# The split words of w_val and w_out come back on SyncE's queue, under a newly searched order table

## The chip, the cores and the metric

The kernel runs on one core of a Trainium2 chip. The metric is the device time of one execution in microseconds, as the median of the runs shown; a profiled execution is a run of its own. Engines are named as in the profile: PE (matmul), PEld (its weight load), DVE (VectorE), ACT (ScalarE), POOL (GpSimd) and SP (SyncE, which here only issues transfers).

## What is computed

Windowed attention feeds a channel mix with squared ReLU and a sigmoid gate, and that feeds a gated projection whose gate is a causal convolution of five taps. All is float32 outside; the weights come in as float64.

```python
# q, k, v: (4, 8, 576, 64)
scores = q @ k^T / sqrt(64), kept where 0 <= row - col < 64
x = softmax(scores) @ v                         # to (4, 576, 512)
xk = mu_k * x + (1 - mu_k) * x_prev;  xr = mu_r * x + (1 - mu_r) * x_prev
v = relu(xk @ w_k) ** 2 @ w_v                   # 512 -> 1024 -> 512
x = sigmoid(xr @ w_r) * v
gate = sigmoid(sum over k of conv_w[k] * xp[:, k:k + S, :])
out = (gate * (x @ w_val)) @ w_out
```

## The kernel before

**Stages.** The 2304 tokens (4 batches of 576) are cut into block 0 of 256 and blocks 1 to 4 of 512. For each block the attention of four head pairs (units) is computed, then the mix: `r` (4 tiles of 128 columns), `h` (8 tiles) and `v` (4 tiles). Results of a block are stored to `x2d` in device memory (`st`). The last stage goes by batch: it loads x of a batch (`ldx`, tile `xb`) and the batch's gate (`ldg`, tile `gate`), multiplies by `w_val` (`val`) and by `w_out` (`out`).

**Split words.** A float32 product is made of three faster ones: both sides are split into a high word and a low word, and high x high, high x low and low x high are summed. A high word is a copy with rounding (`xhi_`, `ghi_`, on ACT or DVE), a low word the difference (`xlo_`, `glo_`, on DVE). In the last stage a product over quarters is made by seven instead of eight products (`m1` to `m7`; each is a group of 12 matmuls on PE), which needs sums of quarters of x and of the weights (`xsum`, tile `xt`). Batch 3's `out` is a plain product of 8 groups, so the stage has 28 + 21 + 8 = 57 groups.

**The weights of the last stage.** During blocks 3 and 4 the quarters of `w_val` and `w_out` are made into their split words (`w_val ld` to `w_val st`) and written to device memory. They come back when the room of the earlier weights is free: `wv2` loads the words of `w_val` into `wk` (after the last `h`), `wo2` those of `w_out` into `wr` (after the last `r`) and into `wol0` and `wol1`. These six loads are issued by POOL.

**Early gates.** For batches 0 to 2 the gate is computed ahead, six half batches in all: load x (`cld`), five taps for each of two column tiles (`ctap`, tile `early`, the first on ACT, the others on DVE), a sigmoid (`cgate`, ACT), store (`cst`, to `gd`).

**What sets the order.** `SLOT` is a table that gives each step a place in one order for all engines, and each engine runs its own steps in that order; a letter before a number says which engine takes a step that may run on either (`a` ACT, `v` DVE, `p` POOL). The order was found by a search with the step lengths that are written at the steps. SP runs its transfers in order too: one that waits holds those behind it. A transfer waits for the producers of its data and for the readers of the room that it fills. So `ldx` of batch 0 waits for POOL's memset of `xb`, and that of batch 1 for the end of `v` in block 4, since its room is that of `wv`.

Of the kernel before, what the change touches and what calls it, by code (L numbers as in the profile page):

```python
# [26 lines left out]
NF = DM // P  # L27
NFF = DFF // P
# [3 lines left out]
NB = len(BLOCKS)  # L32
# [1169 lines left out]
```

## Time and profile before

| what | value |
|---|---|
| median of 3 runs | 429.45 us (429.11 to 430.32) |
| the profiled execution | 432.7 us, span of its instructions 430.9 us |
| mean granted TensorE clock | 0.984 |
| busy, share of the span | PE 96%, DVE 82%, ACT 59%, POOL 4% |
| moved by the 16 DMA engines | 77.69 MB, 180 GB/s in the mean |

The span runs from the first to the last instruction; the time has something around it. Matmuls are pipelined and their ends are modelled, so a busy PE is not yet a PE at full pace.

### The profile page before, as it was taken

What the parts mean: (1) busy time and instruction counts of PE and PEld (TensorE: products, weight loads), DVE (VectorE), ACT (ScalarE), POOL (GpSimd) and SP (SyncE); (2) the same over time, 40 slices, a digit from 0 to 9 for tenths busy, and PEclk for the clock granted to TensorE, in tenths of its full rate; (3) what the DMA queues carried; (4) which work ended last, traced back from release to release, by engine and by line L of the source; (5) the groups of instructions that cost most, each with busy time, mean ns of one, the idle gap of its engine ahead of it and who ended that gap; (6) DMA issues with size and microseconds to landing.
All of it is one profiled execution on the core that took longest, in us unless ns stands there. A gap on an engine that the chain in (4) does not pass through costs nothing.

```text
span 430.9 us, 9154 instructions
## 1 busy us (share of the span) xinstructions
PE 415.3 (96%) x3744; PEld 356.5 (83%) x3744; DVE 355.4 (82%) x524; ACT 253.5 (59%) x579; POOL 19.2 (4%) x67
## 2 busy tenths in 40 slices
PE   7899999999999999999999999999993999999996
PEld 6588888888888888888888888888883999999996
DVE  4899999879987899598989899597239699999970
ACT  5899997888956487761128642334211458675731
POOL 2000000000000000000000000001100000001000
PEclk9799999999999999999999999999997899999999
DMA  7998931452331725401384473529994803607533
GB/s 276 368 418 316 364 109 50 124 181 66 138 104 57 251 76 175 136 20 50 123 300 142 180 257 146 208 106 386 364 351 151 331 1 111 192 2 193 110 140 137
DMA packets 24714, 77.69 MB, mean 180 GB/s; under 512 B 2528, under 2 KB 3296, under 8 KB 22624
## 3 DMA queue, kind: packets, MB, share of 16 engines
q1 hardware_dynamic: 23088, 66.88, 43.5%
q0 software_dynamic: 1440, 10.22, 7.5%
q8 instruction: 29, 0.48, 0.4%
q14 instruction: 13, 0.11, 0.1%
q10 hardware_dynamic: 144, 0.00, 0.0%
HBM read 53.90 MB, written 20.84 MB: 173 GB/s over the span
## 4 chain that ended last, share of the span: by engine, by line
PE 72%; DVE 19%; DMA 6%; issue 1%; ACT 1%; SPq 0%; ACTq 0%; POOL 0%; DVEq 0%; POOLq 0%
PE h L592 18%; PE v L592 15%; PE r L592 8%; DMA xb<-x2d 4%; PE at L501 4%; PE at L489 4%; PE scores L428 4%; DVE x L759 4%; PE v L615 3%; PE h L615 3%; PE out L967 3%; PE val0m L861 2%; PE out2m L861 2%; DVE early L792 2%; DVE gq L759 2%; DVE xt L749 2%
## 5 line engine op out<-in xcount | busy, mean ns | idle before, releaser
L592 PE MATMUL h<-x,wk 128*128 128x512 f32 x384 | 90.5, 392 | 0.0
L592 PEld LDWEIGHTS h<-x,wk 128*128 128x128 f32 x384 | 71.4, 188 | 14.7
L592 PE MATMUL v<-sh,wv 128*128 128x512 f32 x256 | 82.7, 394 | 0.0
L592 PEld LDWEIGHTS v<-sh,wv 128*128 128x128 f32 x256 | 48.1, 188 | 9.9
L592 PE MATMUL v<-sl,wv 128*128 128x512 f32 x128 | 49.8, 389 | 0.0
L792 DVE SCALAR_TENSOR_TENSOR early<-early,wc 128x576 f32<-128x576 f32 x48 | 38.6, 813 | 11.3 <-ACT early L790 11.1
L592 PE MATMUL r<-x,wr 128*128 128x512 f32 x192 | 45.4, 392 | 0.0
L592 PEld LDWEIGHTS r<-x,wr 128*128 128x128 f32 x192 | 35.7, 188 | 7.3
L471 ACT ACTIVATE s<-s,m 128x128 f32<-128x128 f32 x96 | 37.1, 389 | 7.1 <-DVE m L460 7.0
L592 PEld LDWEIGHTS v<-sl,wv 128*128 128x128 f32 x128 | 24.1, 188 | 4.7
L489 PE MATMUL at<-ident,s 128*128 128x128 f32 x144 | 23.8, 288 | 1.9 <-DVE s L481 1.0
L501 PEld LDWEIGHTS at<-pt,vt 128*64 128x64 f32 x576 | 19.2, 141 | 7.2 <-issue 3.4
L489 PEld LDWEIGHTS at<-ident,s 128*128 128x128 f32 x144 | 16.9, 143 | 7.2 <-issue 1.4
L501 PE MATMUL at<-pt,vt 128*64 128x64 f32 x576 | 22.2, 229 | 0.5 <-DVE pt L495 0.5
L481 DVE TENSOR_TENSOR s<-s,m 128x1024 f32<-128x1024 f32 (+1 forms) x20 | 22.3, 1114 | 0.2
L552 DVE SCALAR_TENSOR_TENSOR xm<-xT,omu,xm 128x512 f32<-128x512 f32 x32 | 22.3, 745 | 0.1
L672 DVE TENSOR_TENSOR sl<-rk,sh 128x1024 fp32r<-128x1024 f32 x16 | 19.4, 1220 | 3.2 <-ACT rk L670 3.1
L642 ACT ACTIVATE rk<-h 128x512 f32<-128x512 f32 (+1 forms) x25 | 12.8, 541 | 13.6 <-PE h L592 8.7
L861 PE MATMUL val0m<-x,wk 128*128 128x288 f32 x84 | 14.1, 333 | 7.0 <-DVE x L759 7.0
L756 ACT ACTIVATE x<-xt 128x576 fp32r<-128x576 f32 x15 | 10.1, 681 | 18.1 <-issue 11.5
L861 PEld LDWEIGHTS val0m<-x,wk 128*128 128x128 f32 x84 | 13.6, 224 | 7.4 <-DVE x L759 7.3
L575 DVE TENSOR_TENSOR x<-xm,x 128x1024 fp32r<-128x1024 f32 x16 | 19.3, 1219 | 0.2
(186 smaller groups left out, 844.7 us busy)
## 6 DMA issues: line engine op xcount, KB each, us to landing
qk<-qk SPq DMA_DIRECT2D x16, 544.0 KB, 5.3
vt<-vh SPq DMA_DIRECT2D x16, 512.0 KB, 4.7
xb<-x2d SPq DMA_DIRECT2D x4, 1152.0 KB, 7.4
out_t<-st SPq DMA_DIRECT2D x15, 288.0 KB, 2.5
x2d<-sgs SPq DMA_DIRECT2D x16, 256.0 KB, 3.4
w_out<-w SPq DMA_DIRECT2D x8, 512.0 KB, 2.6
w_val<-w SPq DMA_DIRECT2D x8, 448.0 KB, 2.6
wk<-w_val POOLq DMA_DIRECT2D x2, 1792.0 KB, 10.3
```

Of the source, the lines that this page charges most:

```text
L471: ACT.activation(out=s, in_=scores()[:, c // n2, c % n2, :] if by_pe else s, func=AF.Exp, scale=D ** -0.5 if by_pe else 1.0, bias=l(0)[:, ...
L481: lambda: V.tensor_tensor(out=a["s"], in0=a["s"], in1=l(1).unsqueeze(2).to_broadcast(sq), op=ALU.mult))
L489: PE.transpose(a["tp", h][:, c * P:(c + 1) * P], a["s"][:, h * n2 + c, :], ident)
L501: PE.matmul(a["o"][heads[h], c * W:(c + 1) * W], lhsT=a["v"][:, c, heads[h]], rhs=a["pt"][:, h, c * W:(c + 1) * W], start=True, stop=True)
L552: V.scalar_tensor_tensor(out=m, in0=xT[:, f, :n], scalar=omu[:, c:c + 1], in1=m, op0=ALU.mult, op1=ALU.add)
L575: lambda E: E.tensor_tensor(out=dst(1), in0=src(), in1=f32(dst(0)), op=ALU.subtract))
L592: PE.matmul(ps, lhsT=a, rhs=b[:, kt, :], start=(kt == 0 and i == 0), stop=(kt == nk - 1 and i == 2))
L615: PE.matmul(Ps[key][:, :n], lhsT=ws(kt), rhs=x()[:, kt, :], start=kt == 0, stop=kt == nk - 1)
L672: lambda E: E.tensor_tensor(out=Ss[t][1][:, f, :n], in0=rk(), in1=f32(Ss[t][0][:, f, :n]), op=ALU.subtract))
L759: lambda E: E.tensor_tensor(out=lo(), in0=src(), in1=f32(hi()), op=ALU.subtract))
L792: V.scalar_tensor_tensor(out=o, in0=x, scalar=c, in1=o, op0=ALU.mult, op1=ALU.add)
L861: PE.matmul(z[bank][:, j, :HS], lhsT=lhs, rhs=rhs, start=new and kt == 0 and e == 0, stop=kt == 1 and e == 2, skip_group_check=not new)
```

## The change

The six loads `wv2` and `wo2` are issued by SP in place of POOL, as copies of float32 into a float32 view of the tile. The length that the search took for the scores is 965 ns for blocks 1 to 4 and 411 ns for block 0, where it was 822 ns and half of that. With both the table was searched anew, and nearly all of its numbers differ; of these the diff shows the lines that the text speaks of.

```diff
-    'ldc': '161',
+    'ldc': '17',
...
-    'w_v hi': 'a371 a353 a307 a280',
+    'w_v hi': 'a320 v396 a437 a276',
...
-    'wv2': '870 872',
-    'wo2': '898 904 900 902',
-    'ldx': '893 943 958 1015',
+    'wv2': '891 901',
+    'wo2': '944 900 890 946',
+    'ldx': '886 942 960 1009',
...
-        op(("qk", u), "pe", 822 * nc_ // 8 + (208 if t == 0 else 241) * by_pe, [("ldqk", u), *(["low"] if by_pe else []), *([] if t else ["idle"])], qk,
+        op(("qk", u), "pe", (965 if t else 411) + (208 if t == 0 else 241) * by_pe, [("ldqk", u), *(["low"] if by_pe else []), *([] if t else ["idle"])], qk,
...
-        op(("wv2", c), "pool", 1000, stored("w_val", c) + [("h", NB - 1, m) for m in range(NFF)],
-           lambda c=c: G.dma_start(out=flat(wk[c])[:, :14 * 256], in_=flat4(wd["w_val", c])), moves=1.25 * 14 * 256)
+        op(("wv2", c), "dma", 420, stored("w_val", c) + [("h", NB - 1, m) for m in range(NFF)],
+           lambda c=c: DMA.dma_start(out=f32(flat(wk[c])[:, :14 * 256]), in_=flat4(wd["w_val", c])), moves=1.25 * 14 * 256)
         for j in range(2):
-            op(("wo2", c, j), "pool", 1000, stored("w_out", c) + ([("turn_w", j)] if c else [("r", NB - 1, m) for m in range(NF)]),
-               lambda c=c, j=j: G.dma_start(out=Q["wol", j] if c else flat(wr[j]),
+            op(("wo2", c, j), "dma", 420, stored("w_out", c) + ([("turn_w", j)] if c else [("r", NB - 1, m) for m in range(NF)]),
+               lambda c=c, j=j: DMA.dma_start(out=f32(Q["wol", j] if c else flat(wr[j])),
                                               in_=flat4(wd["w_out", c])[:, j * 2048:(j + 1) * 2048]), moves=1.25 * 2048)
```

The line numbers of the changed kernel are one higher than before from the scores on. In the order's rows `xb_3285` and `xb_3254` are x of batch 0, `xb_3452` and `xb_3451` that of batch 1.

**SP's queue from the last store of split words to x of batch 1.** Before:

```order
L1109 DMA w_out_106<-w_2608 128x1024
L779 DMA early<-x2d 128x2x576
L798 DMA gd<-early 128x2x576
L724 DMA xb_3285<-x2d 128x4x576
L808 DMA gate_3245<-gd 128x4x576
L798 DMA gd<-early 128x2x576
L697 DMA x2d<-sgs 128x512
L724 DMA xb_3452<-x2d 128x4x576
```

Now, from the store of the gate on:

```order
L799 DMA gd<-early 128x2x576
L725 DMA xb_3254<-x2d 128x4x576
L809 DMA gate_3237<-gd 128x4x576
L1121 DMA wol_3058<-w_out_106 128x2048
L1118 DMA wk_63<-w_val_103 128x3584
L1121 DMA wr_66<-w_out_105 128x2048
L1118 DMA wk_64<-w_val_104 128x3584
L698 DMA x2d<-sgs 128x512
L799 DMA gd<-early 128x2x576
L725 DMA xb_3451<-x2d 128x4x576
L1121 DMA wr_65<-w_out_105 128x2048
L1121 DMA wol_3277<-w_out_106 128x2048
```

Four of the loads stand between the gate of batch 0 and the sixth gate's store, two behind x of batch 1.

**The end of the fifth early gate, on DVE** (`early<-early,wc` is a tap, `rk<-h` a rectify, `rk<-rk` the square's product, `sl` its low word, `w<-s` the words of w_out). Before, its eight taps and what lies between:

```order
L792 SCALAR_TENSOR_TENSOR early<-early,wc 128x576 x2
L1106 TENSOR_TENSOR w_2608<-s_3046,w_2570 128x1024
L792 SCALAR_TENSOR_TENSOR early<-early,wc 128x576
L672 TENSOR_TENSOR sl<-rk,sh 128x1024
L644 TENSOR_SCALAR rk<-h_5_3147 128x512
L792 SCALAR_TENSOR_TENSOR early<-early,wc 128x576 x2
L644 TENSOR_SCALAR rk<-h_6_3184 128x512
L792 SCALAR_TENSOR_TENSOR early<-early,wc 128x576
L669 TENSOR_TENSOR rk<-rk 128x1024
```

Now, from the product of the block's first square on:

```order
L670 TENSOR_TENSOR rk<-rk 128x1024
L673 TENSOR_TENSOR sl<-rk,sh 128x1024
L793 SCALAR_TENSOR_TENSOR early<-early,wc 128x576
L1095 TENSOR_TENSOR s_3019<-s_3019 128x128
L1107 TENSOR_TENSOR w_2627<-s_2980,w_2588 128x1024
L793 SCALAR_TENSOR_TENSOR early<-early,wc 128x576
L645 TENSOR_SCALAR rk<-h_4_3112 128x512
L793 SCALAR_TENSOR_TENSOR early<-early,wc 128x576 x4
L1107 TENSOR_TENSOR w_2627<-s_3019,w_2588 128x1024
L793 SCALAR_TENSOR_TENSOR early<-early,wc 128x576
L673 TENSOR_TENSOR sl<-rk,sh 128x1024
L793 SCALAR_TENSOR_TENSOR early<-early,wc 128x576
```

The last tap stood behind the rectify of h tile 6; the next row of the new order is that rectify.

**The same place on ACT, up to the first copies of batch 0's x** (`sh<-rk` is a square, `early<-early` the gate's sigmoid, `sgs<-r` that of r, `x<-xb` and `x<-xt` high words of x). Before:

```order
L666 ACTIVATE sh<-rk 128x1024 x2
L670 ACTIVATE rk<-rk 128x1024
L796 ACTIVATE early<-early 128x1152
L682 ACTIVATE sgs<-r_1_3271 128x512
L682 ACTIVATE sgs<-r_2_3219 128x512
L682 ACTIVATE sgs<-r_3_3254 128x512
L790 ACTIVATE early<-early,wc 128x576 x2
L756 ACTIVATE x<-xt 128x576 x2
```

Now:

```order
L671 ACTIVATE rk<-rk 128x1024 x2
L797 ACTIVATE early<-early 128x1152
L667 ACTIVATE sh<-rk 128x1024
L683 ACTIVATE sgs<-r_0_3206 128x512
L683 ACTIVATE sgs<-r_1_3241 128x512
L757 ACTIVATE x<-xb_3254 128x1152
L791 ACTIVATE early<-early,wc 128x576
L757 ACTIVATE x<-xb_3254 128x576
L683 ACTIVATE sgs<-r_2_3278 128x512
L757 ACTIVATE x<-xt 128x576
L683 ACTIVATE sgs<-r_3_3263 128x512
```

The gate's sigmoid moved ahead of the last square, and three copies of x and a tap stand among r's sigmoids.

**x of batch 0 on DVE** (`xt` are sums, CAST a high word, `x<-..,x` a low word; `x<-xb,x 128x1152` is the one that the stage's first product waits for, `sgs<-v` the product with v). Before:

```order
L749 TENSOR_TENSOR xt<-xb_3285 128x576
L757 CAST x<-xb_3285 128x1152
L792 SCALAR_TENSOR_TENSOR early<-early,wc 128x576
L757 CAST x<-xb_3285 128x576
L749 TENSOR_TENSOR xt<-xt,xb_3285 128x576
L759 TENSOR_TENSOR x<-xb_3285,x 128x576
L792 SCALAR_TENSOR_TENSOR early<-early,wc 128x576
L694 TENSOR_TENSOR sgs<-v_3_3326,sgs 128x512
...
L694 TENSOR_TENSOR sgs<-v_0_3290,sgs 128x512
L759 TENSOR_TENSOR x<-xb_3285,x 128x1152
```

Now:

```order
L750 TENSOR_TENSOR xt<-xb_3254 128x576
L758 CAST x<-xt 128x576
L750 TENSOR_TENSOR xt<-xt,xb_3254 128x576
L760 TENSOR_TENSOR x<-xt,x 128x576
L793 SCALAR_TENSOR_TENSOR early<-early,wc 128x576
L750 TENSOR_TENSOR xt<-xb_3254,xt 128x576
L793 SCALAR_TENSOR_TENSOR early<-early,wc 128x576 x3
L760 TENSOR_TENSOR x<-xt,x 128x576
L750 TENSOR_TENSOR xt<-xb_3254 128x576
L760 TENSOR_TENSOR x<-xb_3254,x 128x1152
```

The low word that the first product needs stood behind three of the four products with v, and stands ahead of all four.

## Rows read from the trace of the kernel before

**Rows 1.** Windows: us, busy of each engine (x instructions), clock, DMA share, GB/s

```profile
core 0: us, PE busy (x) PEld busy (x) DVE busy (x) ACT busy (x) POOL busy (x), PEclk, DMA share, GB/s
0.00:22.00 22.00, 17.67 (x377) 12.93 (x378) 14.63 (x37) 14.66 (x59) 3.21 (x16) 0.85 0.88 324
22.00:323.60 301.60, 301.60 (x2684) 249.79 (x2684) 251.04 (x359) 183.75 (x436) 11.88 (x44) 1.00 0.52 185
305.00:310.00 5.00, 5.00 (x23) 4.14 (x23) 2.21 (x3) 1.45 (x2) 0.00 (x0) 1.00 1.07 417
323.60:331.20 7.60, 0.59 (x4) 0.23 (x2) 7.53 (x12) 1.85 (x2) 0.11 (x1) 0.89 0.34 116
329.50:336.30 6.80, 5.14 (x21) 5.14 (x22) 3.99 (x6) 1.10 (x2) 0.43 (x1) 0.50 0.97 323
331.20:427.20 96.00, 95.42 (x683) 93.58 (x683) 82.25 (x120) 52.67 (x82) 4.04 (x6) 0.97 0.45 139
331.70:337.00 5.30, 5.30 (x26) 5.30 (x25) 1.93 (x4) 0.65 (x1) 0.43 (x1) 0.57 0.98 340
337.00:414.20 77.20, 76.75 (x564) 75.15 (x563) 75.82 (x111) 49.28 (x76) 3.61 (x5) 1.00 0.43 127
```

**Rows 2.** The chain that ended last, in order of time: start, us, what

```profile
294.63 0.59 ACT rk L642
295.22 1.90 ACT sh L666 x2
...
298.11 1.16 ACT early L796
...
299.88 19.01 DMA xb<-x2d
...
324.96 1.55 DVE early L792 x2
...
327.11 1.34 DVE x L759 x2
...
329.84 1.28 DVE x L759
...
414.25 12.83 PE out L967 x96
```

**Rows 3.** Timeline: start, us, engine, line, operation, tiles [idle before, releaser]

```profile
3.08 0.43 SPq L405 DMA_DIRECT2D vt<-vh  x1
...
8.67 0.40 ACT L471 ACTIVATE s<-qk,m 128x128 f32<-128x128 f32 x1
...
290.79 1.27 POOL L1117 DMA_DIRECT2D wk<-w_val  x2 [90.66 <-PE h L592]
291.22 11.04 PE L592 MATMUL r<-x,wr 128*128 128x512 f32 x48
...
297.46 2.36 DVE L672 TENSOR_TENSOR sl<-rk,sh 128x1024 fp32r<-128x1024 f32 x2
...
302.30 1.57 ACT L682 ACTIVATE sgs<-r 128x512 f32<-128x512 f32 x3 [3.03 <-PE r L592]
302.33 0.53 POOL L1120 DMA_DIRECT2D wr<-w_out  x1 [9.50 <-PE r L592]
...
324.08 0.11 POOL L723 MEMSET xb<- 128x16 f32 x1 [19.63 <-PE v L592]
...
328.66 0.94 SPq L724 DMA_DIRECT2D xb<-x2d  x1
```

**Rows 4.** The line that loads x of a batch, and its transfers' time to landing

```profile
L724 SPq DMA_DIRECT2D xb<-x2d x4: 523/574/942, 299.9 to 355.8; - x4
...
DMA to landing us min/median/max: 5.8/7.4/19.0
```

**Rows 5.** DMA issues: tiles, engine, operation, count, KB each, median us to landing

```profile
cw<-conv SPq DMA_DIRECT2D x1, 20.0 KB, 4.6
```

225 rows, old and new, of the table SLOT are left out of this document.

## The prediction

> **What bounds the kernel now.** I read the windows first. From 22 to 323.6 us PE is busy in all of 301.60 us, and VectorE in 251 of them; so until then the kernel is PE's [rows 1]. A busy PE is no proof of full pace, so I took that from the timeline: r's 48 matmuls in 11.04 us, 2.76 us for a group of 12 [rows 3]. Then comes the one large hole: between 323.6 and 331.2 us PE works 0.59 of 7.60 us [rows 1]. The chain of waits says what ended it: the load of batch 0's x (xb<-x2d), issued at 299.88 and 19.01 us under way, then VectorE's steps one behind the other, up to the low word of 1152 columns at 329.84, after which PE goes on [rows 2]. Loads of x landed in 7.4 us in the median [rows 4]. What lay beside this one: POOL issued the two wk loads at 290.79 and the w_out loads from 302.33 on [rows 3], and the engines moved 417 GB/s from 305 to 310 us [rows 1]. So x wasn't late for its own size; it shared a full link with weights that nobody could use before x was there.
>
> Behind the hole PE's clock stands at 0.50 (1.2 of 2.4 GHz) from 329.5 to 336.3 us, after it had done nothing for 7.5 us [rows 1]. From 331.2 to 427.2 us PE runs the last stage: 57 groups of 12, 684 matmuls, 12.83/96 = 0.134 us each in the final run [rows 2], 91.4 us of work in 96.0. Of the 4.6 us over, half clock up to 336.3 costs 5.1/2 = 2.6, and short waits the other 2.0. VectorE is as full as PE there: 75.82 against 76.75 us busy of 77.20 [rows 1].
>
> **The copies.** Six loads leave POOL's queue for SP's. Their sizes follow from the shapes in the order's rows, four bytes a number: wk 1792 KB twice, wr and wol 1024 KB four times; xb and gate 1152 KB each, a gd store 576. On SP they stand behind xb0 and gate0, no longer ahead, so what shares the link with xb0 is one early load and one gd store of 576 KB.
>
> When does xb0 go out? SP holds it behind the gd store of the fifth early gate, which waits for ACT's sigmoid (1.16 us from 298.11 [rows 2]). In the new order that gate's last tap stands on VectorE ahead of the rectify of h tile 6, and the sigmoid on ACT ahead of the last square. Tile 1 of the last block's h has five groups behind it until r begins at 291.22 [rows 3]: it ends at 291.2 - 5 x 2.76 = 277.4. A rectify and a square on ACT (0.59, 1.90/2 [rows 2]) bring VectorE's product to 278.9. From there to the last tap the order has five passes over 1024 columns (1.28 x 1024/1152 = 1.14), eight taps (1.55/2), a rectify (0.6) and a small subtraction (a quarter of a 576 step, 0.2) [rows 2]: 12.7 us. The tap is done at 291.6, the sigmoid at 292.8, xb0 goes out 0.6 behind that, as now: 293.4. For what VectorE itself may wait I add 1: 294.4, 5.5 us earlier than now. Its landing is bounded by 5.8 and 19.0; I take 7.4, the median, since it stands alone at the front of its queue and POOL's is empty [rows 4]: 301.8.
>
> From there VectorE has, up to the low word that the first product needs, four sums and two low words of 576 columns (1.34/2), a rounding (at most as much), four taps and the low word of 1152 (1.28) [rows 2]: 9.1 us, done at 310.9. It has the time: after the last slo at 299.82 [rows 3] it works 2.21 us from 305 to 310 [rows 1]. PE's last group of v ends at 323.6, so x has 12 us to spare. If that cover were gone, each us would be PE's.
>
> The weights: gd, xb0, gate0, wol0, wk0, wr1, wk1 are 576 + 2 x 1152 + 2 x 1024 + 2 x 1792 = 8512 KB, 8.7 MB in one line from about 294 us. At 417 GB/s that is 20.9 us, 314.9; at the 323 GB/s of 329.5 to 336.3 it is 27.0, 321 [rows 1]. PE wants wk at 323.6: in time either way, and I count nothing. On SP wr1 waits for the end of r at 302.26 and wk1 stands behind it; on POOL wk waited for h alone and went at 290.79 [rows 3]. But of the 5.8 MB ahead of wr1 at most 8.3 us x 417 GB/s = 3.5 have moved by then, so the link doesn't run dry, and the hold costs nothing. The trace has such a hold: the second xb went out at 328.66, behind a gd store, though its own memset had been free to run since 324.08 [rows 3]. The Trainium skill (DMA: Bandwidth & Descriptors, Anatomy of one DMA) has it as a rule, and it speaks against this change: DMA engines don't wait on semaphores, the issuing sequencer does, before dispatch. By that rule all that stands behind wr1 is held with it; without it wk1 would land at the same 314.9, since the line ahead of it is as long. So it is a rival below and no term.
>
> Behind xb1, which waits for the end of v (324.1), stand wr0 and wol1: with it 3200 KB, 3.3 MB from 324.8, landed at 332.7 or, by 323 GB/s, 335. The first product with w_out was PE's sixth group of the stage and is now the tenth: 323.7 + 9 x 1.6 = 338.1. Free as well; xb1 itself leaves 4 us earlier than now.
>
> **The table.** Of the steps that may run on either engine 62 are on VectorE for 81, and 189 on ACT for 171: relief for VectorE. From 22 to 323.6 us PE can gain nothing, and can lose where its feed comes later: bounds 0 and +2, I take 0, since VectorE's load falls. The scores' length changes no instruction; it only steered the search. In the first 22 us PE works 17.67 us, and half clock is there too (0.85 in the mean [rows 1]); the conv load now takes the second vt's place on SP (3.08 [rows 3]) and lands 4.6 us later [rows 5], at 7.7, before ACT, which unpacks it behind the second unit's exponentials, is done with these at about 9.1 [rows 3]. Bounds -2 and +2, I take 0.
>
> **The sum.** PE doesn't stop at 323.6: -7.5. The half clock loses its cause: up to -2.6. But it was a grace for VectorE too: from the end of its last product with v (331.7) to its last split (414.2) it was busy 1.93 + 75.82 = 77.75 of 82.5 us [rows 1]. It has three steps fewer there now, 1.3 us or so: 76.4 from 324.9, done at 401.3 without any wait, where PE wants that split at 323.7 + 49 x 1.6 = 402.1. Two engines so equal will wait for each other; I let 1.0 of the 2.6 go in that: -1.6. Together -9.1, and the profiled span of 430.9 becomes 421.8. That execution took 432.7 us with what lies around the span, 3.25 above the median of 429.45; the difference goes to the median: 420.4.
>
> **The rivals.** *VectorE holds the stage* (0.14): the same start, but PE waits all through; the stage keeps its 96 us, and with 1 to 2 us more -6 is left: 423.5. *The weights are late* (0.10): if one queue moves less than 323 GB/s, wk1 lands at 326 to 328, PE waits 2 to 4 us and half clock follows: 424 to 426. For it speaks SP's hold, against it the 2.4 MB still in line at 302.3. *The early stretch pays* (0.08): PE's feed comes 5 to 9 us late in sum and the gain is gone, 425 to 430. For it speaks that every engine's order is new, against it the steps that VectorE hands over. *The x load drags the sigmoids* (0.05), the one on the other side: ACT's new order puts first copies of x ahead of r's last two sigmoids, and v's third first half needs the bank that the last one frees. If xb0 lands at L, that sigmoid ends at about L + 4.3 (a step of 1152 columns 1.16, three of half that and a bit at 0.7, two sigmoids of 1.57/3 [rows 2, 3]); PE wants the bank at 302.26 + 2 x 2.76 = 307.8. Nothing is lost up to L = 303.5, then 1 us for 1: at today's 19.0 us L is 313.4, PE stands 10 us in the midst of v and half clock follows: 433. It decides from L = 311 on. My 301.8 leaves 1.7 us, so a loss of one or two is in my range.
>
> **How the numbers follow.** My forecast has 0.63, from 417.5 to 423.5. The whole range goes down to 416.8 (all of 2.6 back, and 2 of the first 22 us) and up to 426.0, with a holding VectorE and late weights inside, and the sigmoids and half of the early case out. A measurement of this kernel tells 0.3% (1.3 us) from no change. Faster: the first three cases and half of the early one, 0.91; same 0.03; slower 0.06, the sigmoids and the tail of the early case.
>
> **What would show it.** In the profile of the changed kernel: xb0 issued near 294 and landed by 303; no hole in PE over 1 us at the end of v; the clock at 1.00 through the last stage; VectorE's sums of x before 311; wk landed before v's end. I'd be wrong with a wait of PE on wk at the stage's start, on a sigmoid within v, or with holes before 320 us.

## The result, and the profile after

The changed kernel took **424.88 us** in the median of 4 runs (422.71 to 426.11), the kernel before beside it 429.28 (428.92 to 430.32): ratio 0.9888, 95% interval 0.9843 to 0.9933, so faster by about 1%; a second comparison below, with more runs, has 0.9841. The profiled execution took 424.55 us, its span 422.8. Forecast were 420.4 us and a range of 416.8 to 426.0: the time lies in the range, but the gain is 4.4 us and not 9.1.

The windows of the changed kernel; they answer to [rows 1].

```profile
0.00:22.00 22.00, 16.04 (x356) 11.65 (x356) 13.41 (x37) 14.45 (x59) 2.80 (x15) 0.88 0.84 298
22.00:326.00 304.00, 304.00 (x2713) 251.48 (x2706) 251.19 (x347) 192.62 (x454) 12.88 (x40) 1.00 0.51 181
323.60:331.20 7.60, 7.60 (x51) 7.17 (x50) 4.46 (x7) 0.18 (x1) 0.22 (x2) 1.00 0.59 211
326.10:422.10 96.00, 91.93 (x684) 91.03 (x682) 81.31 (x117) 53.48 (x84) 3.94 (x7) 1.00 0.51 166
337.00:414.20 77.20, 77.20 (x578) 76.85 (x577) 72.07 (x105) 48.04 (x75) 3.72 (x5) 1.00 0.48 149
```

Where PE worked 0.59 of 7.60 us it now works all of them, and the clock stays at 1.00 through the last stage. In 337.0 to 414.2 us PE is busy in every microsecond. VectorE has 72.07 us there where it had 75.82, but the stage began earlier behind v and this stretch holds other parts of it; like is compared with like further down. The first 22 us went the other way: PE works 16.04 us there, 1.63 less than before.

The chain of waits (start, us, what), for all of the span and, from 6.85 to 15.58, for its first 25 us:

```profile
6.85 7.66 DMA x<-w_r
...
14.65 0.93 issue
15.58 0.42 ACT pt L495
...
304.31 21.76 PE v L593 x96
326.06 7.25 PE val0m L862 x54
...
406.02 12.81 PE out L968 x96
```

The load of x is no longer in the chain: v's last matmul hands over to the first product with `w_val`.

Timeline of the changed kernel, the places that the prediction named; they answer to [rows 2, 3]:

```profile
14.54 1.18 ACT L339 ACTIVATE words<-x 128x1024 f32<-128x1024 f32 x1 [1.56 <-DMA x<-w_r]
16.05 0.44 PE L490 MATMUL at<-ident,s 128*128 128x128 f32 x2 [3.19 <-ACT pt L495]
...
23.95 1.03 PE L616 MATMUL r<-x,words 128*128 128x256 f32 x4
...
293.26 11.04 PE L593 MATMUL r<-x,wr 128*128 128x512 f32 x48
296.18 0.61 SPq L725 DMA_DIRECT2D xb<-x2d  x1
303.87 0.76 DVE L750 TENSOR_TENSOR xt<-xb 128x576 f32<-128x576 f32 x1 [4.63 <-DMA xb<-x2d]
304.34 0.32 SPq L1121 DMA_DIRECT2D wr<-w_out  x1
304.70 0.43 SPq L1118 DMA_DIRECT2D wk<-w_val  x1
306.16 0.58 ACT L683 ACTIVATE sgs<-r 128x512 f32<-128x512 f32 x1
312.40 1.35 DVE L760 TENSOR_TENSOR x<-xb,x 128x1152 fp32r<-128x1152 f32 x1
...
325.90 8.25 PE L862 MATMUL val0m<-x,wk 128*128 128x288 f32 x60
```

The same three places in the kernel before (w_r's first piece unpacked, the first matmul of r, the first of the last stage):

```profile
13.55 1.18 ACT L338 ACTIVATE words<-x 128x1024 f32<-128x1024 f32 x1 [0.64 <-DMA x<-w_r]
...
21.99 2.02 PE L615 MATMUL r<-x,words 128*128 128x256 f32 x8
...
323.86 0.29 PE L861 MATMUL val0m<-x,wk 128*128 128x288 f32 x1
```

The first step on x begins 7.7 us behind the load's issue, where the load alone took 19.01, and the low word that the stage waits for is done at 313.75, 12 us ahead of need. The first product with `w_val` stands at 325.90; from there the stage takes 92.9 us (it ends at 406.02 + 12.81 = 418.83), where behind the hole it took 96.0. From that product to the end of the span it is 422.8 - 325.90 = 96.9 us; before, where it stood at 323.86, 430.9 - 323.86 = 107.0. So 10.1 us are gained. But the stage begins 2.0 us later, and the chain says where that comes from: a load of w_r in the first 15 us, ACT behind it, PE behind that. The lines that load x and wk, by their times to landing, answer to [rows 4]:

```profile
L725 SPq DMA_DIRECT2D xb<-x2d x4: 517/572/1225, 296.2 to 347.8; - x4
...
DMA to landing us min/median/max: 5.7/6.7/16.2
...
L1118 SPq DMA_DIRECT2D wk<-w_val x2: 432/659/886, 298.9 to 304.7; - x2
...
DMA to landing us min/median/max: 15.2/15.6/16.1
```

The last wk landed by 304.7 + 16.1 = 320.8, before the first product.

### The profile page after: what moved, and what is told of

The parts are those of the page before. It is cut to its first block, busy times and chain, and to the rows that moved or that the text cites. A ratio compares the mean times of both kernels' runs of the same rounds, so it can differ in the third digit from the quotient of the medians.

```text
span 422.8 us, 9154 instructions
## 1 busy us (share of the span) xinstructions
PE 412.1 (97%) x3744; PEld 354.3 (84%) x3744; DVE 345.9 (82%) x501; ACT 260.6 (62%) x597; POOL 19.6 (5%) x62
## 4 chain that ended last, share of the span: by engine, by line
PE 96%; DMA 2%; issue 1%; DVE 0%; ACT 0%; SPq 0%; ACTq 0%; POOL 0%; DVEq 0%; POOLq 0%
PE h L593 21%; PE v L593 21%; PE r L593 10%; PE at L502 4%; PE at L490 4%; PE scores L429 3%; PE v L616 3%; PE h L616 3%; PE out L968 3%; PE out2m L862 3%; PE val3m L862 3%; PE val1m L862 3%; PE out1m L862 3%; PE val2m L862 3%; PE out0m L862 3%; PE val0m L862 3%
## 5 line engine op out<-in xcount | busy, mean ns | idle before, releaser
L593 PE MATMUL h<-x,wk 128*128 128x512 f32 x384 | 91.5, 393 | 0.0
L495 ACT ACTIVATE pt<-at 128x512 f32<-128x512 f32 (+1 forms) x32 | 17.5, 566 | 14.6 <-PE at L490 14.6
L490 PEld LDWEIGHTS at<-ident,s 128*128 128x128 f32 x144 | 16.8, 143 | 9.7 <-ACT pt L495 3.4
L695 DVE TENSOR_TENSOR sgs<-v,sgs 128x512 f32<-128x512 f32 (+1 forms) x20 | 12.7, 634 | 12.0 <-PE v L593 11.9
L443 DVE SCALAR_TENSOR_TENSOR s<-scores,cap 128x1024 f32<-128x1024 f32 x12 | 14.6, 1218 | 9.5 <-PE at L490 9.5
L643 ACT ACTIVATE rk<-h 128x512 f32<-128x512 f32 (+1 forms) x29 | 15.1, 546 | 8.7 <-PE h L593 7.0
```

The lines of the kernel that those rows point to most:

```text
L490: PE.transpose(a["tp", h][:, c * P:(c + 1) * P], a["s"][:, h * n2 + c, :], ident)
L495: ("act", p_ns(n), lambda h=h: ACT.activation(out=a["pt"][:, h, :n], in_=a["tp", h][:, :n], func=AF.Copy)),
L593: PE.matmul(ps, lhsT=a, rhs=b[:, kt, :], start=(kt == 0 and i == 0), stop=(kt == nk - 1 and i == 2))
```

## The experiments

Theory 1: the hole came from two queues that shared the link; on one line x comes first, so the move of the six loads is the whole gain and the table adds nothing. Rivals: the table makes the gain; or x was slow for its own rows.

**The kernel before, unchanged.**

> The kernel before, unchanged, profiled again. The execution whose trace the prediction used took 432.7 us, 3.3 above the median of its runs. If that is what every profiled execution has over a plain one, this trace has the same span near 431 us, the clock at 0.984 and both stretches of half clock; if that execution was a long one of a spread, the span is near 427.5 us and something is missing in it, the second half clock or a part of the hole at the end of v.

Measured: 431.26 us, as the kernel before beside it (431.42). Its profiled execution took 428.55 us, span 426.8. Windows and timeline of it:

```profile
0.00:22.00 22.00, 16.58 (x384) 12.44 (x384) 15.93 (x39) 16.24 (x67) 3.31 (x16) 1.00 0.89 327
322.30:327.40 5.10, 0.28 (x2) 0.00 (x1) 5.07 (x8) 1.85 (x2) 0.11 (x1) 0.75 0.50 170
324.90:331.70 6.80, 4.30 (x18) 4.30 (x19) 4.84 (x7) 1.34 (x2) 0.43 (x1) 0.50 0.96 313
```

The hole is there again, 5.1 us long in place of 7.6, with half clock from 324.9 us on; but the first 22 us have a clock of 1.00, where [rows 1] show 0.85. So the execution of [rows 1 to 3], 432.7 us, was a long one, by its hole and by its start.

**The six loads alone,** under the old table at the places that they had:

```diff
-        op(("wv2", c), "pool", 1000, ...
-           lambda c=c: G.dma_start(out=flat(wk[c])[:, :14 * 256], ...
+        op(("wv2", c), "dma", 420, ...
+           lambda c=c: DMA.dma_start(out=f32(flat(wk[c])[:, :14 * 256]), ...
...   (and the same for wo2)
```

> The kernel before with nothing but the six loads moved to SP's queue, at their old places in the old order: wk stands ahead of xb0 there, the w_out loads behind gate0. Theory 1 (the hole came from sharing the link with a second queue): in one line xb0 has the whole link once wk has landed; issued near 300 it lands by 306 to 308, the low word that the first product needs is done near 323, the hole of 7.5 us shrinks to under 1 us and the last stage keeps its full clock; as the start is the old one, about 422 us, 7 below before and some 2 below the changed kernel. Theory 2 (the new order did it, by issuing xb0 5 us earlier and putting that low word ahead of the products with v): the hole stays above 5 us and the time within 2 us of before.

Measured: 423.82 us (423.04 to 425.11), ratio 0.9841 (0.9801 to 0.9881). Timeline:

```profile
292.32 0.90 SPq L1117 DMA_DIRECT2D wk<-w_val  x2
301.65 0.61 SPq L724 DMA_DIRECT2D xb<-x2d  x1
310.95 0.75 DVE L749 TENSOR_TENSOR xt<-xb 128x576 f32<-128x576 f32 x1
323.96 1.35 DVE L759 TENSOR_TENSOR x<-xb,x 128x1152 fp32r<-128x1152 f32 x1
325.67 8.15 PE L861 MATMUL val0m<-x,wk 128*128 128x288 f32 x60
```

Though wk goes 9 us ahead of x, x lands within 9.1 us, the low word is done at 325.3, and PE goes from v to `val0m` without a hole. The moves alone are the gain; the new table takes 0.7 us more off the last stage (97.6 us to the span's end here, 96.9 in the changed kernel, table below) and gives a reserve: the low word is done 0.4 us before PE wants it here, 12 us before in the changed kernel.

**The table alone,** the changed kernel with the six loads back on POOL (the diff above in reverse).

> The changed kernel with the six loads put back on POOL's queue, everything else as changed. Theory 1: xb0 shares the link again with one wol and one wk load that POOL issues before it, and takes 11 to 15 us instead of 7.7; it lands at 308 to 311, r's last sigmoid ends 4 us behind that, and PE stands 2 to 5 us within v; 427 to 430 us. Theory 2: as the changed kernel within 1 us.

Measured: 440.13 us (438.59 to 441.87), ratio 1.0222 (1.0173 to 1.0272). Timeline:

```profile
296.95 0.62 SPq L725 DMA_DIRECT2D xb<-x2d  x1
...
320.02 1.16 ACT L757 ACTIVATE x<-xb 128x1152 fp32r<-128x1152 f32 x1 [19.75 <-DMA xb<-x2d]
322.33 0.57 ACT L683 ACTIVATE sgs<-r 128x512 f32<-128x512 f32 x1
322.96 0.80 PE L593 MATMUL v<-sh,wv 128*128 128x512 f32 x1 [12.44 <-ACT sgs L683]
```

and its DMA queues from 296 to 320 us (packets, MB, share; q0 is POOL's, q1 SP's):

```profile
q0 software_dynamic: 576, 5.77, 62.7%
q1 hardware_dynamic: 1435, 3.20, 37.9%
```

x needs 23.0 us beside POOL's 5.77 MB, not the 11 to 15 expected. ACT holds r's sigmoids behind it, and PE stands 12.44 us in the midst of v, not 2 to 5: the prediction's rival of the sigmoids, in full. Of the changed kernel's table that is the price that only the SP line hides.

**The same with r's last two sigmoids ahead of the copies of x.**

```diff
-    'sig': '... 780 888 894 907 912',
+    'sig': '... 780 888 894 897.1 897.2',
```

> The new table with the six loads on POOL, as in the second experiment (440.13 us, PE stood 12.6 us in the midst of v), with one move more: r's last two sigmoids stand on ACT ahead of the first copies of batch 0's x. Theory 1 (x needs about 23 us in any case, since POOL's loads share the link; what made the second experiment slower than the kernel before was only that ACT waited for x ahead of the sigmoids): x lands near 320 again, the sigmoids end by 308, v runs through to about 326, then a hole until x is worked up, 8.5 to 9 us behind x's landing, so of 3 to 6 us, and the time is 428 to 432, like the kernel before. Rival 1 (the new table is slower with POOL's loads at other places too): above 434. Rival 2 (the copies of x go to ACT late enough now that PE waits for products or low words elsewhere in v): a stall inside v of more than 2 us.

Measured: 434.13 us (433.14 to 438.09), ratio 1.0068 (1.003 to 1.0105). Timeline:

```profile
304.57 1.09 ACT L683 ACTIVATE sgs<-r 128x512 f32<-128x512 f32 x2 [4.84 <-PE r L593]
319.16 0.76 DVE L750 TENSOR_TENSOR xt<-xb 128x576 f32<-128x576 f32 x1 [19.70 <-DMA xb<-x2d]
...
328.37 3.33 PE L862 MATMUL val0m<-x,wk 128*128 128x288 f32 x23 [1.95 <-DVE x L760]
335.73 7.25 PE L862 MATMUL val0m<-x,wk 128*128 128x288 f32 x36 [4.02 <-DVE early L875]
```

v runs through, as theory 1 said, and the hole is back behind it, in two parts: 1.95 us for the low word and 4.02 for VectorE, which then works off what x had held up, together 5.97 where 3 to 6 were expected. The time missed the expected 428 to 432 and reached the 434 of rival 1. The last stage isn't why, it has 106.8 us to the span's end, like the 107.0 of [rows 1] (table below); r begins 2.2 us later than there (24.18 against 21.99). So ACT's order decides where PE waits, 12.44 us within v or 5.97 behind it; that it waits comes from the late x.

**wk ahead of x on SP.**

```diff
-    'wv2': '891 901',
+    'wv2': '885.1 885.2',
```

> The changed kernel with the two wk loads (3.67 MB) on SP ahead of batch 0's x in place of behind it; every other step stands as in the changed kernel. Theory 1 (a queue moves its transfers one behind the other): x lands by as much later as the two loads take, 3.67 MB / 417 GB/s = 8.8 us, so at 312 to 313 in place of 303.9; r's last sigmoid ends 4 us behind that, near 316.7, where PE wants its bank at about 310; PE stands some 6 to 7 us in the midst of v, the clock may fall to half behind it, and the time is 430 to 435. Rival 1 (transfers of one queue share the link like those of two queues): x lands at 318 to 321, PE stands 12 us, the time is near 440. Rival 2 (x's load is bound by its own rows and not by what stands ahead of it): x lands by 306, PE stands at most 1 us in v, and the time is that of the changed kernel, 424 to 426.

Measured: 433.46 us (430.73 to 434.55), ratio 1.0046 (1.0007 to 1.0084). Timeline:

```profile
297.56 1.76 SPq L1118 DMA_DIRECT2D wk<-w_val  x2
299.49 0.71 SPq L725 DMA_DIRECT2D xb<-x2d  x1
...
301.27 6.35 SPq L1121 DMA_DIRECT2D wol<-w_out  x1
...
313.71 0.76 DVE L750 TENSOR_TENSOR xt<-xb 128x576 f32<-128x576 f32 x1 [12.93 <-DMA xb<-x2d]
316.69 0.79 PE L593 MATMUL v<-sh,wv 128*128 128x512 f32 x1 [5.40 <-ACT sgs L683]
```

x lands at 313.7, 9.8 us later than in the changed kernel, for 3.67 MB more ahead of it (8.8 us at 417 GB/s) and a start of r 0.7 later. The second wk landed by 310.7 (issued at 298.1, 12.6 us under way), x 3.0 us behind it, which is 1.18 MB at 393 GB/s. So here the queue moved its transfers one behind the other, and where x stands in the line decides. With the loads alone under the old table wk stood ahead of x too, but went out at 292.3, early enough.

**The first 25 us.** In the changed kernel ACT unpacks w_r's first piece (1024 KB) ahead of a copy of transposed scores (`pt`) for which PE waits; SP's line has conv (the taps, 20 KB), then that piece, then the second vt (a unit's v, 256 KB). In the kernel before it has that vt, then the piece, and conv later. Six kernels, all with the changed kernel's tail, take this apart: `pt` first (the SLOT values of the second unit's `pt` below those of `w_r g`):

```diff
-    'pt': 'v35 a46 a61 v62 ...
+    'pt': 'v35 a46 a54 v61.5 ...
-    'w_r g': '54 85',
-    'w_r t': '59 101',
+    'w_r g': '61 85',
+    'w_r t': '62 101',
```

> The changed kernel with two pairs of steps exchanged in the first 20 us: ACT copies the second unit's first transposed tile (pt 1 0) before it unpacks the first piece of w_r, and VectorE the second tile before its shift of that piece; in the changed kernel both wait there for the piece, which lands at 14.5 us, and PE waits 3.4 us for the tile. Theory 1: the end of v moved from 323.6 to 326.1 us by this wait, so 2 to 3 us come back: PE's wait near 12.6 us is under 1 us, v ends by 324.3, and the time is 422 to 423 us. Rival: the first products with w_r wait for the piece itself, which lands no earlier, so they start at the same 23.9 us and the time stays within 0.7 us of the changed kernel.

conv late again (`'ldc': '160.5'`, `'wc0': '434.5 329.5 460.5'`, `'wc': '462.5'`):

> The changed kernel with the conv load and the three steps that unpack it back at the places they had before (the load behind the second unit's vt, the unpacking in block 2). In the changed kernel the first piece of w_r lands at 14.54 us where it landed at 13.55 before, PE stands 3.35 us at 12.6 us and r begins at 23.95. Theory 1 (the early conv load takes a place on SP and time on ACT, so the piece and the transposes behind it come late): the piece lands near 13.6, that stall shrinks to 2.4 us or less, r begins near 23.0, v ends 0.9 us earlier, near 325.2, and the time is some 0.9 us below the changed kernel's. Rival (the piece is late for its own issue, 1.27 us on SP, and conv's few bytes have no part): the piece lands at 14.4 to 14.6, the stall stays between 3.0 and 3.4 and v ends at 326.0.

both edits:

> The changed kernel with both edits of the first 25 us: the order of the third experiment (the copies of transposed scores ahead of the unpacking of w_r's first piece) and the conv load at its place of before. Theory 1 (the two delays add): r begins near 22.0, where it began before, v ends near 324.2, 1.9 us before the changed kernel's, and the time is 422.0 to 422.8, 0.4 to 0.7% below the changed kernel's 424.88 and under the kernel before by 1.5% or more. Rival (the third experiment's gain and that of the conv load are the same wait, or the rest of the span takes the time back): v ends at 325.0 to 325.3 and the time is that of the third experiment, 423.8.

both, and idle matmuls in PE's waits:

```diff
+    'pad': '52.5 60.5 66.5',
...
+    for i, n in enumerate((5, 5, 14)):
+        op(("pad", i), "pe", n * 112, [("exp", 3)], lambda n=n: pad(n))
```

> The sixth experiment (both edits of the first 25 us) with 24 idle matmuls of 128 columns on zeros more, 5, 5 and 14, put into PE's three waits between 12.6 and 16.8 us (0.70, 0.52 and 1.87 us there); they write a bank that the second half of block 0's scores has left, and nothing reads them. An idle matmul takes 0.112 us at full clock (6.194 to 6.864 us, 6 of them). Theory 1 (these waits let the clock fall, and the half clock of 3 to 10 us behind them is what puts r's begin later and makes it vary; the runs with no and with 3.4 us of half clock have r at 20.46 and 21.40): the clock stays at 1.00 until r, r begins at 20.5 to 21.5, the last stage begins near 323 and the time is 421 to 422, under the changed kernel by 0.6% or more. Rival (the clock falls for another cause in the first 20 us, or PE is held by what it waits for, not by its own pace): a half-clock stretch of 6.8 us or more as before, r at 22.8 to 24, and a time of 423.5 to 425.

both, and the second vt ahead of the piece (`'w_r ld': '24.5 43'` for `'23 43'`), without and with idle matmuls (5, 5, 5):

> The sixth experiment (both edits of the first 25 us) with the second unit's vt (256 KB) on SP ahead of the first piece of w_r (1024 KB) again, as it stood before; in the changed kernel it stands behind the conv load and that piece. In the eighth experiment, where nothing else held PE there, PE waited 1.87 us for this vt, to 17.18 us. Theory 1 (the changed kernel begins r later because this vt lands behind the piece): PE's wait at 15 us on the product of the second unit is gone or below 0.5 us, r begins at 21 to 22.5, and the time is 422 to 423. Rival (the piece, which lands 0.6 us or more later for it, is what PE and VectorE wait for then; or the clock falls anyway): r begins at 23 to 24.5, the time is 423.5 to 425.5, that of the sixth experiment. The last stage has 96.7 to 97.1 us by both.

> The ninth experiment with the idle matmuls of the eighth, but 5, 5 and 5 in place of 5, 5 and 14: in the eighth each took two passes, the last 14 held PE for 3.39 us (17.80 to 21.02) and the transposes behind them, whose data was there at 19.5 us. Theory 1 (with the vt early and the waits filled neither data nor clock hold PE): the clock stays at 1.00, r begins at 20.5 to 21.5 as in the run of the kernel before that had no half clock (20.46), and the time is 421 to 422.5. Rival (loads that land at other times from execution to execution set r's begin, whatever the order): r at 22.5 or later, and a median within 0.3% of the eighth experiment's 423.55.

and the changed kernel once more beside the kernel before:

> The changed kernel unchanged, beside the kernel before, to see how its first 25 us fall from execution to execution. In the profiles so far with this kernel's order of the first 25 us r begins at 23.95, 24.50, 24.18 and 24.67 us, with 6.8 or 10.2 us of half clock ahead of it; with the order of before at 21.99 and 20.46, with 6.8 us and none. Theory 1 (the span is three terms, r's begin, 301.9 us from there to the last stage, 96.9 us of last stage): r begins between 23.5 and 24.8, the last stage has 96.7 to 97.1 us, the span is 422.3 to 423.6 and the median 424.5 to 425.5. Rival (the last stage varies too, as it does in the kernel before, 107.0 and 104.5 us): its length is off 96.9 by more than 0.5 us.

All in one table, from the timelines and the granted clock of each profiled execution: when ACT begins to unpack the piece, how long the clock is at half in the first 30 us, r's first matmul, the last stage's first matmul, and what is left of the span from there.

| kernel | median us | profiled us | unpack | half clock | r | stage | rest |
|---|---|---|---|---|---|---|---|
| before, [rows 1] | 429.28 | 432.7 | 13.55 | 6.8 | 21.99 | 323.86 | 107.0 |
| before, again | 431.26 | 428.55 | 12.82 | none | 20.46 | 322.30 | 104.5 |
| changed | 424.88 | 424.55 | 14.54 | 6.8 | 23.95 | 325.90 | 96.9 |
| changed, again | 425.57 | 426.96 | 15.43 | 10.2 | 25.29 | 328.31 | 96.9 |
| loads alone | 423.82 | 425.11 | 15.94 | 6.8 | 23.91 | 325.67 | 97.6 |
| table alone | 440.13 | 440.51 | 15.09 | 6.8 | 24.50 | 341.50 | 97.2 |
| sigmoids first | 434.13 | 434.67 | 14.73 | 6.8 | 24.18 | 326.13 | 106.8 |
| wk first | 433.46 | 434.11 | 14.87 | 10.2 | 24.66 | 335.44 | 96.9 |
| pt first | 423.83 | 423.85 | 14.41 | 6.8 | 22.79 | 325.19 | 96.9 |
| conv late | 425.83 | 422.15 | 12.48 | 3.4 | 21.39 | 323.50 | 96.9 |
| both | 423.88 | 425.42 | 13.24 | 10.2 | 23.38 | 326.76 | 96.8 |
| both, filled | 423.55 | 425.26 | 14.90 | none | 24.30 | 326.60 | 96.9 |
| vt first | 424.58 | 424.93 | 15.91 | 6.8 | 24.26 | 326.23 | 96.9 |
| vt first, filled | 424.18 | 424.08 | 15.14 | none | 22.09 | 325.40 | 96.9 |

Ratios to the kernel before, with intervals: changed, again 0.9841 (0.9809 to 0.9872); pt first 0.9838 (0.98 to 0.9877); conv late 0.9841 (0.9783 to 0.99); both 0.9815 (0.9768 to 0.9862); both, filled 0.9801 (0.9775 to 0.9827); vt first 0.984 (0.9795 to 0.9885); vt first, filled 0.9847 (0.9811 to 0.9883).

What follows. The rest is 96.9 us, within 0.1, in every kernel with the loads on SP and the new table: the tail is settled. The head isn't. The changed kernel once more had r at 25.29, outside the 23.5 to 24.8 that were expected. Behind the unpacking r begins 7.6 to 8.4 us later in the three executions of the old table, and 9.4 to 9.9 in the five that have the changed kernel's head. With `pt` first it is 8.4 again (22.79 - 14.41): that order costs about 1 us as far as one execution shows (conv late, with the changed kernel's order, has 8.9), and not the 2 to 3 that I had expected back. The other part goes with the time at which the piece lands. With conv early the unpacking began at 14.41 to 15.43 us (six executions, 14.85 in the mean). With conv late it began at 12.48, 13.24 and 14.90 where SP's line is otherwise the same (conv late, both, and both, filled), and at 12.82, 13.55 and 15.94 under the old table, whose second vt goes ahead of the piece: 13.82 in the mean of the six, about 1 us earlier, but two of the six were as late as the others, so conv is at most a part of it. Late conv bore theory 1 out in its profiled execution (12.48, r at 21.39), yet its other three took 425.67 to 426.08 us, and a gain in the median isn't shown; with both edits the two gains did not add (r at 23.38, 10.1 behind the unpacking: PE waited there for the vt). With vt first the piece came at 15.91, and PE's wait there went on (3.98 us, for VectorE).

That half clock makes r late holds in part. Both filled kernels keep the clock at 1.00, as theory 1 had it, but r began at 24.30 and 22.09. In the first of them PE waited for the vt, and then spent 3.39 us on idle matmuls (14 in the program, 28 in the trace) where data was there at 19.5; timeline of it:

```profile
17.18 0.69 PE L503 MATMUL at<-pt,vt 128*64 128x64 f32 x16 [1.87 <-DMA vt<-vh]
17.80 3.39 PE L1144 MATMUL pads<-sgs 128*128 128x128 f32 x28
21.02 0.60 PE L491 MATMUL at<-ident,s 128*128 128x128 f32 x4
```

The second began r 22.09 - 15.14 = 7.0 us behind the unpacking, 1.4 less than vt first at half clock, but lost that again before the last stage. Its six runs lie within 1.0 us (424.05 to 425.04), those of the changed kernel within 3.5 (423.43 to 426.96). But the six of both, filled, which had the clock at 1.00 too, lie within 2.8 (422.51 to 425.26), so it isn't shown that the clock in the head makes the spread. No version is shown to beat the changed kernel; the nearest is both, filled, 423.55 against 425.57 side by side, with intervals that overlap.

## Why the prediction was right, and where not

**The hole and its cause: right.** The loads alone gave the gain, the table alone a loss, and with POOL's loads x took 16.8 to 23.0 us in four executions of three kernels. The DMA queues of the kernel before from 308 to 319 us, while x was under way beside POOL's loads (packets, MB, share; q0 is POOL's, q1 SP's):

```profile
q0 software_dynamic: 470, 3.46, 78.2%
q1 hardware_dynamic: 472, 1.05, 27.6%
```

Both queues moved as many packets, but POOL's are over three times as long (7.4 KB against 2.2 in the mean). So SP's queue, with x in it, had 1.05 of 4.52 MB, or 95 GB/s: it lost some three quarters of the link and not a half. The table alone shows the same from 310 to 314 us, 155 packets and 149. The Trainium skill (DMA: Bandwidth & Descriptors, Queues, rings and completion order) says that each DMA engine takes turns between the queue rows that have work, packet by packet; these counts agree. In the changed kernel only one queue has work there, and it moved 2.85 MB in the 7.6 us from x's issue to its landing. Whether loads on a second queue that isn't POOL's would slow x as much, no run shows.

**xb0's issue and landing: right.** Forecast 3.2 us behind r's begin in block 4 (294.4 - 291.2), measured 2.9 (296.18 - 293.26); landing 7.4, measured 7.6; low word 9.1 us behind landing, measured 9.9.

**The weights: right.** wk1 by 321, measured by 320.8; SP stood for r's end (wr1 issued at 304.34, wk1 at 304.70), and PE never waited for a weight. So the hold is there, and the trace agrees with the Trainium skill (DMA: Bandwidth & Descriptors, Anatomy of one DMA), which says that the wait is the issuing sequencer's, before dispatch; it cost nothing.

**The last stage: right in sign, mis-sized.** I let VectorE keep 1.0 of the 2.6 us of half clock; the stage took 92.9 us, not 96.0 - 1.6 = 94.4. Windows from VectorE's last product with v to the end of its last step, before and now:

```profile
331.70:418.40 86.70, 86.25 (x620) 84.65 (x619) 81.75 (x119) 50.62 (x78) 4.04 (x6) 0.97 0.46 141
326.80:409.70 82.90, 82.11 (x612) 81.46 (x611) 80.62 (x116) 50.81 (x79) 3.72 (x5) 1.00 0.55 175
```

VectorE has three steps fewer and 1.1 us less to do, about as counted (1.3). The term that was off is the wait between two engines as full as these: PE waits for VectorE nowhere in the stage now, though VectorE is busy in 80.62 of 82.90 us; its one wait is 0.8 us for ACT, at the start. So all of the 2.6 came back, and half a us of the short waits with it. The rival by which VectorE holds the stage fell. (The split at 414.2 that I called VectorE's last is the one on which `out` starts; two follow.)

**The first 22 us: the term that failed.** "I take 0", with bounds of 2: r began 2.0 us later in the profile and 3.3 in the second one. I had looked at the conv load, which ACT had unpacked from 9.01 us on without harm, and not at w_r's piece: its unpacking stands ahead of `pt`, and it lands later. Of the 2.0 about 1 is that order; the other goes with the landing, 1 us later in the mean with conv early, but so different from execution to execution (15.94 even under the old table) that the cause stays open. From r to the last stage it was 301.87 us before and 301.95 after: the 0 there was right.

**From span to median: wrong.** I took the 3.25 us by which the profiled execution lay above the median as something around the span. It was the length of that one execution: its hole was 7.6 us, in the other profile 5.1, and its start had half clock, the other's had none. So I took a long execution's hole off the median of shorter ones; from the second profile the tail gives 104.5 - 96.9 = 7.6 us, not 10.1. The sum was 421.8 and 422.8 was measured, but the median is 424.88 and not 420.4: 3.25 for the base, 1.0 for the span (2.0 lost at the head, 1.0 more gained in the tail: 10.1 for 9.1), and 0.3 since this profiled execution lies below its median. That the time lies in the range is in part luck: the upper end was there for a holding VectorE and for late weights, and neither came; the base and the head took the room. The lower end doesn't add up: 420.4 less 1.0 and 2 is 417.4, not 416.8.

**The rival of the sigmoids: a mechanism that is real, and mis-priced.** Two kernels showed it. PE goes on 2.9 to 3.0 us behind x's landing (322.96 - 320.02, 316.69 - 313.71), not 4.3: it waits for the third sigmoid, not the last. The changed kernel had that one at 306.7, where PE wanted the bank at 304.3 + 2 x 2.76 = 309.8: 3.1 us to spare. With POOL's loads the table would have lost as I priced it (433 forecast, 440 measured, with a late head and 13.7 us of half clock, 4.5 of them behind the stop).

## What to carry over

When a small load on the critical path crawls, look first at what another queue moves meanwhile: one line with the urgent load in front took 8 to 10 us off the tail here (104.5 and 107.0 to 96.9), and the same line with 3.7 MB more in front gave some 8 of them back in the middle of v (433.46 us against 424.88 and 425.57). Beside a queue with longer packets it is not a half of the link that is lost: here three quarters were. A table that is searched for one placement of the loads can be worth 2% less than nothing under another. And split an execution at the points where one engine becomes the bound (here r's begin, the last stage's begin, the end) before summing: here the last part repeats within 0.1 us where the whole spreads by 3.

## What was not expected of the hardware

SP's issue of a DMA is not of one length, and the load's landing goes with it. Leaving out the two kernels with the vt moved, the issue of w_r's first piece took 0.43 us in four executions, and the piece landed in 6.3 to 7.1 us; in eight it took 1.22 to 1.83 us, and the piece landed in 7.5 to 9.1. What lengthens it the runs don't show. The longest issue was 6.35 us (`wol<-w_out` with wk first), with 7.2 MB issued in the 5.3 us ahead of it. PE's clock fell in the head for 3.4, 6.8 or 10.2 us, or not at all, in executions of nearly the same program; it stayed at 1.00 in the profiles of both kernels that had idle matmuls in waits of 0.5 to 1.9 us, and in one profile of the kernel before, which has none.
